# A depth-first forward pass in a fixed order on every engine, for a four-layer training step on one core

## The chip, the cores and the metric

One core of a Trainium2 chip runs the whole program, as one launch. The metric is the device time of that launch in microseconds (us). The core has a matrix engine (TensorE, here PE, with a separate row PEld for its weight loads), VectorE (DVE), ScalarE (ACT), GpSimd (POOL), and queues that issue DMAs; the one of SyncE (SP) issues nearly all of them here, ACT's a few.

## The reference

The input is one sequence of 2048 tokens with 512 features in bf16. Four layers follow one another: A, B, A, B, and both A layers share their weights, as do both B layers. The program returns the output and the gradients of the input and of the five weight matrices.

```
def _A_ref(x, wqkv, wo):
    H = 32; Dh = D // H
    qkv = (x @ wqkv).reshape(B, S, 3, H, Dh).transpose(2, 0, 3, 1, 4)
    q, k, v = qkv[0], qkv[1], qkv[2]
    phi = lambda t: jnp.where(t > 0, t + 1, jnp.exp(t)) + 1e-6
    pq, pk = phi(q), phi(k)
    kv = jnp.einsum("bhsd,bhse->bhde", pk, v)
    z = jnp.einsum("bhsd->bhd", pk)
    num = jnp.einsum("bhqd,bhde->bhqe", pq, kv)
    den = jnp.einsum("bhqd,bhd->bhq", pq, z)[..., None] + 1e-6
    return (num / den).transpose(0, 2, 1, 3).reshape(B, S, D) @ wo

def _B_ref(x, w_gate, w_up, w_down):
    g = jnp.einsum("bsd,df->bsf", x, w_gate)
    u = jnp.einsum("bsd,df->bsf", x, w_up)
    return jnp.einsum("bsf,fd->bsd", _sigmoid(g) * u, w_down)

x = x + _A_ref(_layernorm(x), A_wqkv, A_wo)
x = x + _B_ref(_layernorm(x), B_w_gate, B_w_up, B_w_down)
x = x + _A_ref(_layernorm(x), A_wqkv, A_wo)
x = x + _B_ref(_layernorm(x), B_w_gate, B_w_up, B_w_down)
```

F, the inner width of B, is 1376: ten chunks of 128 and one of 96. In A, kv and z are sums over all tokens, so no output of A can be made before every token's k and v are there.

## The kernel before

The tokens are 16 tiles of 128, or 4 blocks of 512. The residual stream stays in SBUF in f32 (one tile x per 128 tokens), and what the backward pass needs is stored to DRAM (sv_...). Layers 0 to 3 run one after the other.

The forward pass of an A layer (a_fwd) has three stages. First, for each tile: the layer norm (statistics on DVE, the reciprocal root in two small POOL operations, L291 and L292, the scaling on ACT, L295), four PE transposes into hT (L303), twelve wide matmuls for q, k and v (L402), two Exp on ACT, the min and max steps of phi on DVE, the copy of v on ACT, four more transposes of pq into pqT_all with an ACT copy, and stores of pq, pk and v by blocks. Second, once all tiles are through, z (L432) and kv (L438) are summed on PE in a stretch of their own. Third, for each tile: num and den (L455, L458), the division on DVE (L464), four transposes (L303) with an ACT copy to oT (L312), the product with wo (L476), a copy from PSUM on ACT (L479) and the residual add on POOL (L480).

The forward pass of a B layer (b_fwd) goes block by block: for each chunk of F four matmuls for g and four for u (L553, L556), two Sigmoid on ACT (L558, L560; the second is of -g), a product on DVE (L561) and one on POOL (L562). The product with w_down (L533) and the residual add on DVE (L535) of the block before are woven in at four chunks, together with the layer norms of the next block. sg, qg and hh are stored for each block.

The weights are loaded on SP at the start. After the forward pass their buffers are given back, and the backward pass loads transposed weights into that place with DMA transposes on SP (L201, L205, L206), then grad_out tiles. Its two kinds of phases are those that make gradients of activations (b_bwd_p1, a_bwd_p1) and those that make gradients of weights (b_bwd_p2, a_bwd_p2; L781, L811), the latter with transposed loads of p_set on SP (L757). In a_bwd_p1, BatchLoader (L631) loads two tiles of o and of pq at a time, two buffers each; pq is used by a DVE step (L932) and by PE (L921).

The order in which each engine works is chosen by the planner of the language at build time: it takes instructions by priority, in the order of the code, with a cost model, and may pull later ones forward. Within an engine's queue the result is fixed, and an instruction that waits holds all behind it.

Of the kernel before, what the change touches and what calls it, by code (L numbers as in the profile page):

```python
# [17 lines left out]
D = 512  # L18
# [32 lines left out]
def kernel(  # L51
# [43 lines left out]
    def load_stream(io, src2d, b):  # L95
        stg_t = io.tile([P, NB, D], BF16, name="io_in")
        if b == 0:
            nc.sync.dma_start(out=stg_t[:, 0, :], in_=src2d[0:P, :])
            nc.sync.dma_start(out=stg_t[:, 1:NB, :],
                              in_=src2d[P:NB * P, :].rearrange("(n p) d -> p n d", p=P))  # L100
        else:
            nc.sync.dma_start(out=stg_t[:], in_=dram_batch(src2d, b))
        for j in range(NB):
            st = b * NB + j
            if j % 2 == 0:
                nc.vector.tensor_copy(k.xs[st][:], stg_t[:, j, :])
            else:
                nc.scalar.copy(k.xs[st][:], stg_t[:, j, :])
        return stg_t
    k.load_stream = load_stream  # L110

    def store_stream(io, dst2d, b):
        stg_t = io.tile([P, NB, D], BF16, name="io_out")
        for j in range(NB):
            st = b * NB + j
            nc.gpsimd.tensor_scalar(stg_t[:, j, :], k.xs[st][:], 1.0, 0.0, ALU.mult, ALU.add)
        nc.sync.dma_start(out=dram_batch(dst2d, b), in_=stg_t[:])
    k.store_stream = store_stream


    k.sv = {}
    for l in range(4):
        d = {}
        d["h"] = dram.tile([S, D], BF16, name=f"sv_h{l}")
        d["gbf"] = dram.tile([S, D], BF16, name=f"sv_gbf{l}")
        if l % 2 == 0:
            for nm in ("pq", "pk", "v", "o"):
                d[nm] = dram.tile([S, D], BF16, name=f"sv_{nm}{l}")
            d["dqkv"] = dram.tile([S, 3 * D], BF16, name=f"sv_dqkv{l}")
        else:  # L130
            for nm in ("sg", "qg", "hh", "du", "dg"):
                d[nm] = dram.tile([F, S], BF16, name=f"sv_{nm}{l}")
        k.sv[l] = d
# [15 lines left out]
    with tc.tile_pool(name="wfwd", bufs=1) as wfwd:  # L149
        k.wqkv = wfwd.tile([P, NDC, 3 * D], BF16, name="wqkv")  # L150
        with tc.tile_pool(name="io0", bufs=2) as io:
            load_stream(io, x_in, 0)
            nc.sync.dma_start(out=k.wqkv[:], in_=A_wqkv.rearrange("(c p) j -> p c j", p=P))
            for b in range(1, NST // NB):
                load_stream(io, x_in, b)
        k.wo = wfwd.tile([P, NDC, D], BF16, name="wo")
        nc.sync.dma_start(out=k.wo[:], in_=A_wo.rearrange("(c p) j -> p c j", p=P))
        k.wg = wfwd.tile([P, NDC, F], BF16, name="wg")
        nc.sync.dma_start(out=k.wg[:], in_=B_w_gate.rearrange("(c p) j -> p c j", p=P))
        k.wu = wfwd.tile([P, NDC, F], BF16, name="wu")  # L160
        nc.sync.dma_start(out=k.wu[:], in_=B_w_up.rearrange("(c p) j -> p c j", p=P))
        k.wd = wfwd.tile([P, NFC, D], BF16, name="wd")
        nc.sync.dma_start(out=k.wd[:, 0:NFC - 1, :],
                          in_=B_w_down[0:(NFC - 1) * P, :].rearrange("(c p) j -> p c j", p=P))
        nc.sync.dma_start(out=k.wd[0:FLAST, NFC - 1, :], in_=B_w_down[(NFC - 1) * P:F, :])

        with ExitStack() as lctx:
            k.lnres = dict(
                stg=lctx.enter_context(tc.tile_pool(name="ln_stg", bufs=2)),
# [888 lines left out]
```

## Time and profile before

| What | us |
|---|---|
| median of 3 runs | 1398.83 (1398.69 to 1399.06) |
| the profiled execution, its time | 1398.62 |
| the profiled execution, its span | 1396.9 |
| PE busy in the span | 1234.9 (88%) |
| DVE, ACT, POOL busy | 666.1, 497.4, 250.2 |
| first matmul of layer 0 | 21.4 |
| first g matmul of layer 1 | 124.8 |
| first qkv matmul of layer 2 | 251.1 |
| first g matmul of layer 3 | 347.6 |
| last matmul of the forward pass ends | 465.8 |
| first PE work of the backward pass | 493.3 |

The span is the time from the first to the last instruction in the profile; the launch adds about 1.7 us to it. PE is busy for most of the span, but its busy time includes the tail of each pipelined matmul, so the text prices matmuls by the distance between the starts of two that follow one another. A line such as "PE tp L303 <- DVE ostage L464: 6.9, 9, 1.5" says that PE, before the instructions of line 303 that write tp, sat idle for 6.9 us in total in 9 places, the longest 1.5, until a DVE instruction of line 464 had written ostage. In the tables by stretch, the busy times of PE, PEld, DVE, ACT and POOL, each with its count of instructions, are followed by the granted clock of PE (1.00 is full), the busy share of the DMA engines and their GB/s.

### The profile page before, as it was taken

The page shows a single profiled execution, that of the slowest core. Times are in us where ns is not written, and L with a number is a line of the kernel's source. Part 1 is how long each engine was busy: PE and PEld are TensorE (multiplying, and loading weights), DVE is VectorE, ACT ScalarE, POOL GpSimd, SP SyncE. Part 2 cuts the span into 40 slices and gives each one's busy share as a digit, 9 for nine tenths or more (in the row PEclk, how much of TensorE's full clock was granted, in tenths as well). Part 3 has the DMA queues.
Part 4 walks back from the last instruction along what each step waited for, and adds up shares of the span by engine and source line. Part 5 has one row for each costly group of instructions (what it writes and reads, how often), then busy time and mean ns, then how long its engine had stood idle before and what let it go on. Part 6 is the DMA issues. An engine that isn't in the chain of part 4 may idle for free. (4 is left out here: it accounts for less than half of the span.)

```text
span 1396.9 us, 22644 instructions
## 1 busy us (share of the span) xinstructions
PE 1234.9 (88%) x8960; PEld 750.9 (54%) x8960; DVE 666.1 (48%) x1435; ACT 497.4 (36%) x871; POOL 250.2 (18%) x405
## 2 busy tenths in 40 slices
PE   3978999997999389998989889999989999749888
PEld 1454444454444156555745567655567665427657
DVE  6665565667443167666746200567513857301111
ACT  4846554656644122113457211111113457200000
POOL 4027555007644000011000100110101001000000
PEclk9989999999999789999999999999999999979999
DMA  8421355432444999969674897998687874799845
GB/s 279 166 75 62 122 167 192 164 114 91 152 137 137 261 288 304 243 162 254 162 203 137 179 222 160 291 269 229 165 255 226 219 195 164 195 242 214 177 118 157
DMA packets 469323, 263.70 MB, mean 189 GB/s; under 512 B 197728, under 2 KB 463584, under 8 KB 469216
## 3 DMA queue, kind: packets, MB, share of 16 engines
q1 hardware_dynamic: 446752, 247.57, 65.5%
q10 hardware_dynamic: 22464, 14.68, 3.8%
q8 instruction: 70, 1.15, 0.3%
q14 instruction: 37, 0.30, 0.1%
HBM read 98.37 MB, written 117.51 MB: 155 GB/s over the span
## 5 line engine op out<-in xcount | busy, mean ns | idle before, releaser
L781 PE MATMUL p_ps<-p_set,p_a 128*128 128x256 bf16 (+1 forms) x1920 | 210.8, 268 | 34.5 <-DMA p_set<-sv_dg 24.5
L781 PEld LDWEIGHTS <-p_a 128*128 128x128 bf16 x1920 | 173.8, 99 | 64.1 <-DMA p_set<-sv_dg 26.3
L580 ACT ACTIVATE t_sb<-dh_ps,rstd_all 128x512 f32<-128x512 f32 x64 | 44.0, 687 | 202.2 <-issue 114.7
L562 POOL TENSOR_TENSOR qg_t<-hh_t,oms 128x512 bf16<-128x512 bf16 (+1 forms) x88 | 101.1, 1152 | 80.1 <-DVE hh_t L561 74.0
L702 DVE TENSOR_TENSOR du_t<-dhh_ps,sg_ld 128x512 bf16<-128x512 f32 x96 | 61.2, 637 | 109.3 <-PE dhh_ps L700 109.3
L402 PE MATMUL mm_ps<-wqkv,hT 128*128 128x512 bf16 x384 | 94.8, 387 | 1.7 <-DVE x L535 1.7
L811 PE MATMUL p_ps<-p_a,p_set 128*128 128x512 bf16 (+1 forms) x352 | 84.8, 388 | 10.3 <-DMA p_set<-sv_hh 10.3
L561 DVE TENSOR_TENSOR hh_t<-u_ps,sg_t 128x512 bf16<-128x512 f32 (+1 forms) x88 | 60.4, 688 | 69.7 <-PE u_ps L556 50.0
L700 PE MATMUL dhh_ps<-gT,wdT 128*128 128x256 bf16 (+1 forms) x704 | 86.9, 276 | 7.5 <-DVE dg_t L704 6.2
L556 PE MATMUL u_ps<-hT,wu 128*128 128x512 bf16 (+1 forms) x352 | 90.3, 379 | 1.8 <-DVE hh_t L561 1.8
L553 PE MATMUL g_ps<-hT,wg 128*128 128x512 bf16 (+1 forms) x352 | 90.3, 379 | 1.6 <-DVE kvbdT L494 1.6
L582 DVE SCALAR_TENSOR_TENSOR junk<-t_sb,h_ld 128x512 bf16<-128x512 f32 x64 | 44.3, 692 | 96.2 <-ACT t_sb L580 96.2
L584 POOL TENSOR_SCALAR ab<-c 128x2 f32<-128x2 f32 x64 | 12.2, 191 | 418.4 <-DVE junk L582 418.4
L670 PE MATMUL dh_ps<-wuT,du_t 128*128 128x512 bf16 (+1 forms) x352 | 85.3, 383 | 0.3 <-DVE du_t L702 0.3
L670 PE MATMUL dh_ps<-wgT,dg_t 128*128 128x512 bf16 (+1 forms) x352 | 82.1, 380 | 0.0
L533 PE MATMUL y_ps<-wd,hh_t 128*128 128x512 bf16 (+1 forms) x352 | 81.6, 379 | 0.0
L700 PEld LDWEIGHTS <-wdT 128*128 128x128 bf16 (+1 forms) x704 | 68.3, 101 | 23.3 <-DVE dg_t L704 12.7
L610 POOL TENSOR_SCALAR gstage<-x 128x512 bf16<-128x512 f32 x48 | 32.0, 686 | 234.5 <-PE gT_ps L303 129.3
L786 DVE TENSOR_TENSOR dw_stg<-p_ps,dw_stg 128x512 bf16<-128x512 f32 (+1 forms) x36 | 23.5, 654 | 105.3 <-PE p_ps L781 99.9
L558 ACT ACTIVATE sg_t<-g_ps 128x512 bf16<-128x512 f32 (+1 forms) x88 | 52.3, 594 | 55.0 <-PE g_ps L553 54.9
L986 PE MATMUL dh_ps<-wqkvT,dkvT 128*128 128x512 bf16 x256 | 65.6, 380 | 0.0
L480 POOL TENSOR_TENSOR x<-y_sb,x 128x512 f32<-128x512 f32 x32 | 40.2, 1265 | 134.7 <-ACT y_sb L479 134.6
(158 smaller groups left out, 2041.8 us busy)
## 6 DMA issues: line engine op xcount, KB each, us to landing
sv_sg<-sg_t SPq DMA_DIRECT2D x8, 1280.0 KB, 5.7
sv_qg<-qg_t SPq DMA_DIRECT2D x8, 1280.0 KB, 7.8
sv_hh<-hh_t SPq DMA_DIRECT2D x8, 1280.0 KB, 9.2
sg_ld<-sv_sg SPq DMA_DIRECT2D x16, 640.0 KB, 5.5
qg_ld<-sv_qg SPq DMA_DIRECT2D x16, 640.0 KB, 6.3
sv_du<-du_t SPq DMA_DIRECT2D x16, 640.0 KB, 4.1
sv_dg<-dg_t SPq DMA_DIRECT2D x16, 640.0 KB, 5.6
sv_h<-hstage SPq DMA_DIRECT2D x16, 512.0 KB, 4.3
```

Of the source, the lines that this page charges most:

```text
L402: nc.tensor.matmul(ps[:], lhsT=hT[:, kc, :], rhs=k.wqkv[:, kc, n * D:(n + 1) * D], start=(kc == 0), stop=(kc == NDC - 1))
L533: nc.tensor.matmul(y_ps[:], lhsT=T["hh"][0:r, fc, j * P:(j + 1) * P], rhs=k.wd[0:r, fc, :], start=(fc == 0), stop=(fc == NFC - 1))
L553: nc.tensor.matmul(g_ps[0:r, :], lhsT=k.wg[:, kc, fs], rhs=hT[:, kc, :], start=(kc == 0), stop=(kc == NDC - 1))
L556: nc.tensor.matmul(u_ps[0:r, :], lhsT=k.wu[:, kc, fs], rhs=hT[:, kc, :], start=(kc == 0), stop=(kc == NDC - 1))
L561: nc.vector.tensor_tensor(T["hh"][0:r, fc, :], u_ps[0:r, :], T["sg"][0:r, fc, :], ALU.mult)
L562: nc.gpsimd.tensor_tensor(T["qg"][0:r, fc, :], T["hh"][0:r, fc, :], oms[0:r, :], ALU.mult)
L670: nc.tensor.matmul(dh_ps[:], lhsT=T[nm][0:r, fc, j * P:(j + 1) * P], rhs=wT[0:r, fc, :], start=(i == 0), stop=(i == n_mm - 1))
L700: nc.tensor.matmul(dhh_ps[0:r, i, :], lhsT=k.wdT[:, jc, fc * P:fc * P + r], rhs=gT[:, jc, :], start=(jc == 0), stop=(jc == NDC - 1))
L702: nc.vector.tensor_tensor(T["du"][0:r, fp:fp + n, :], dhh_ps[0:r, 0:n, :], sg[0:r, fp:fp + n, :], ALU.mult)
L781: nc.tensor.matmul(psv[:, icl, :], lhsT=lhs_all[:, st, ic * P:(ic + 1) * P], rhs=set_t[:, st, 0:W], start=(st == 0), stop=(st == NST - 1))
L811: nc.tensor.matmul(ps[0:r, :], lhsT=st_t[:, st, j * P:j * P + r], rhs=g_all[:, st, :], start=(st == 0), stop=(st == NST - 1))
L986: nc.tensor.matmul(dh_ps[:], lhsT=lhsT, rhs=k.wqkvT[:, n * NDC + c, :], start=(i == 0), stop=(i == 3 * NDC - 1))
```

## The change

The forward pass is a new class, Forward. Its instructions are issued within a manual schedule: every engine runs them in the order in which the code makes them, with no planner. The backward pass is planned as before.

- Head: the x tiles are loaded into a staging buffer; the layer norm reads that buffer, and POOL makes the f32 copy. The thirds of wqkv for k and v are loaded by ACT's queue, the one for q by SP. A loop staggers the tiles: in step i the statistics of tile i, the scaling of tile i-1, the transposes of tile i-2, the k and v matmuls of tile i-3 and the kv sums of tile i-4.
- kv and z are summed in two PSUM banks that stay open, tile by tile (acc_tile), while k and v are made. For layer 2 this goes on between the blocks of layer 1 (k_block, v_acc).
- q is made by blocks with the weights as the stationary operand, so that it comes out as pqT, 128 features by 512 tokens; it is neither transposed on PE nor kept for the whole sequence. It is stored as pqT.
- phi takes its min step on POOL in place of DVE, 512 columns at a time.
- Depth first: block sb of layer B follows as soon as block sb of layer A is out; o_block of the next block, the kv sums and the last steps of kv are woven between its matmuls. drive() picks, at build time, the stream that is least far along among those whose modelled latency is over, with 217 ns for a wide matmul and 57 for a square one; the second number of each yield is the latency in ns that it assumes.
- The attention's residual add reads PSUM directly on DVE; the ACT copy y_sb and the POOL add are gone.
- All small PSUM tiles share six buffers in turn. sg and qg are stored for every two chunks from a ring of three buffers, hh for each block.
- In a_bwd_p1, pq is loaded from sv_pqT by DMA transposes (TransLoader), two tiles at a time.

gu_block, not shown, has the matmuls, Sigmoids and products of b_fwd; k_tile and v_tile have the k and v matmuls; kv_finish masks the sums into rhsN and kv_extra makes the forms that the backward pass needs.

```diff
-            for nm in ("pq", "pk", "v", "o"):
+            for nm in ("pk", "v", "o"):
                 d[nm] = dram.tile([S, D], BF16, name=f"sv_{nm}{l}")
+            d["pqT"] = dram.tile([D, S], BF16, name=f"sv_pqT{l}")
...
-            lns = [FwdLN(k, l) for l in range(4)]
-            a_fwd(k, 0, lns[0], nxt=lns[1])
-            b_fwd(k, 1, lns[1], nxt=lns[2])
-            a_fwd(k, 2, lns[2], nxt=lns[3])
...
-            b_fwd(k, 3, lns[3], out_cb=out_cb)
+    with ExitStack() as fctx:
+        Forward(k, fctx, x_in, A_wqkv, A_wo, B_w_gate, B_w_up, B_w_down, out0).run()
...
+def drive(streams, t=0.0):
+    live = [dict(g=g, tot=tot, done=0.0, ready=t) for g, tot in streams]
+    while live:
+        ok = [s for s in live if s["ready"] <= t]
+        s = min(ok, key=lambda s: s["done"] / s["tot"]) if ok else min(live, key=lambda s: s["ready"])
+        t = max(t, s["ready"])
+        try:
+            cost, lat = next(s["g"])
+        except StopIteration:
+            live.remove(s)
+            continue
+        t += cost
+        s["done"] += cost
+        s["ready"] = t + lat
...
+        self.p_hh = pool("f_hh", 2)
+        self.p_ring = pool("f_ring", 3)
+        self.ps = pool("f_ps", 6, space=PSUM)
...
+    def phi(self, dst, ps):
+        nc = self.nc
+        e_t = self.p_ea.tile([P, D], BF16, name="e_t")
+        nc.scalar.activation(e_t[:], ps, ACT.Exp)
+        a_t = self.p_e2.tile([P, D], BF16, name="a_t")
+        nc.gpsimd.tensor_scalar(a_t[:], e_t[:], 1.0, EPS, ALU.min, ALU.add)
+        return lambda: nc.vector.scalar_tensor_tensor(dst, ps, 1.0 + EPS, a_t[:], ALU.add, ALU.max)
+    def q_block(self, l, sb):
+        nc = self.nc
+        hT = self.hA.pop((l, sb))
+        t = self.p_pq.tile([P, NDC, SB], BF16, name="pqT")
+        self.pq[l, sb] = t
+        late = None
+        for c in range(NDC):
+            ps = self.ps_tile("q_ps")
+            for kc in range(NDC):
+                nc.tensor.matmul(ps[:], lhsT=self.wqkv[:, kc, c * P:(c + 1) * P], rhs=hT[:, kc, :],
+                                 start=(kc == 0), stop=(kc == NDC - 1))
+            nxt = self.phi(t[:, c, :], ps[:])
+            if late is not None:
+                late()
+            late = nxt
+            yield NDC * MM, 0
+        late()
+        yield 0, 3000
+        nc.sync.dma_start(out=self.k.sv[l]["pqT"][:, sb * SB:(sb + 1) * SB].rearrange("(c p) s -> p c s", p=P),
+                          in_=t[:])
...
+    def acc_tile(self, l, st):
+        k, nc = self.k, self.nc
+        sb, j = divmod(st, NB)
+        pk, v = self.kvt[l, sb]
+        last = st == NST - 1
+        for c in range(NDC):
+            cs = slice(c * P, (c + 1) * P)
+            nc.tensor.matmul(self.kv_ps[:, c, :], lhsT=pk[:, j, cs], rhs=v[:, j, cs], start=False, stop=last,
+                             skip_group_check=True)
+            nc.tensor.matmul(self.z_ps[:, c:c + 1], lhsT=pk[:, j, cs], rhs=k.ones_col[:], start=False, stop=last,
+                             skip_group_check=True)
...
+    def o_tile(self, l, st):
+        k, nc = self.k, self.nc
+        sb, j = divmod(st, NB)
+        kv = k.kv[l]
+        pq = self.pq[l, sb][:, :, j * P:(j + 1) * P]
+        if j == 0:
+            self.ost = self.p_o.tile([P, NB, D], BF16, name="ostage")
+        ost = self.ost
+        num = self.ps_tile("num_ps")
+        den = self.ps_tile("den_ps", (P, H))
+        for c in range(NDC):
+            nc.tensor.matmul(den[:, c * 8:(c + 1) * 8], lhsT=pq[:, c, :], rhs=kv["rhsN"][:, c, P:P + 8],
+                             start=True, stop=True)
+            nc.tensor.matmul(num[:, c * P:(c + 1) * P], lhsT=pq[:, c, :], rhs=kv["rhsN"][:, c, 0:P],
+                             start=True, stop=True)
+        rden = kv["rden_all"][:, st, :]
+        dtmp = self.small.tile([P, H], F32, name="dtmp")
+        nc.vector.tensor_scalar(dtmp[:], den[:], EPS, None, ALU.add)
+        nc.vector.reciprocal(rden, dtmp[:])
+        o_t = ost[:, j, :]
+        nc.vector.tensor_tensor(o_t.rearrange("p (h e) -> p h e", h=H), num[:].rearrange("p (h e) -> p h e", h=H),
+                                rden.unsqueeze(2).to_broadcast([P, H, DH]), ALU.mult)
+        yield NDC * 84, 1800
+        tp = self.ps_tile("o_tp", (P, NDC, P), BF16)
+        for c in range(NDC):
+            nc.tensor.transpose(tp[:, c, :], o_t[:, c * P:(c + 1) * P], k.ident[:])
+        oT = self.p_oT.tile([P, NDC, P], BF16, name="oT")
+        nc.scalar.copy(oT[:], tp[:])
+        if j == NB - 1:
+            nc.sync.dma_start(out=dram_batch(k.sv[l]["o"], sb), in_=ost[:])
+        yield NDC * TR, 1000
+        y = self.ps_tile("y_ps")
+        for c in range(NDC):
+            nc.tensor.matmul(y[:], lhsT=oT[:, c, :], rhs=self.wo[:, c, :], start=(c == 0), stop=(c == NDC - 1))
+        nc.vector.tensor_tensor(k.xs[st][:], y[:], k.xs[st][:], ALU.add)
+        yield NDC * MM, 1000
+        yield from self.ln(l + 1, st, k.xs[st][:])
+        yield from self.hT(l + 1, st)
+        if j == NB - 1:
+            self.store_h(l + 1, sb)
...
+    def o_block(self, l, sb):
+        gens = [self.o_tile(l, sb * NB + j) for j in range(NB)]
+        live = []
+        ready = {}
+        t = 0.0
+        while gens or live:
+            if gens and len(live) < 3:
+                g = gens.pop(0)
+                live.append(g)
+                ready[id(g)] = t
+            g = min(live, key=lambda g: (ready[id(g)]))
+            wait = max(0.0, ready[id(g)] - t)
+            if wait > 0:
+                yield 0, wait
+            t += wait
+            try:
+                c, lat = next(g)
+            except StopIteration:
+                live.remove(g)
+                continue
+            t += c
+            ready[id(g)] = t + lat
+            yield c, 0
...
+    def y_block(self, l, sb, last=False):
+        k, nc = self.k, self.nc
+        pend = []
+        if last:
+            ot = self.p_o.tile([P, NB, D], BF16, name="out0_t", tag="ostage")
+        for j in range(NB):
+            st = sb * NB + j
+            self.y_tile(l, st)
+            yield NFC * MM, 0
+            if last:
+                nc.scalar.copy(ot[:, j, :], k.xs[st][:])
+                continue
+            pend.append(self.ln(l + 1, st, k.xs[st][:]))
+            for g in list(pend):
+                try:
+                    next(g)
+                except StopIteration:
+                    pend.remove(g)
+        self.hh.pop((l, sb))
+        if last:
+            yield 0, 2000
+            nc.sync.dma_start(out=dram_batch(self.out0, sb), in_=ot[:])
+            return
+        while pend:
+            yield 0, 2000
+            for g in list(pend):
+                try:
+                    next(g)
+                except StopIteration:
+                    pend.remove(g)
+        yield 0, 1000
+        for j in range(NB):
+            yield from self.hT(l + 1, sb * NB + j)
+        self.store_h(l + 1, sb)
...
+        load_x(0)
+        for n in (1, 2):
+            nc.scalar.dma_start(out=self.wqkv[:, :, n * D:(n + 1) * D], in_=self.w_in["wqkv"][:, :, n * D:(n + 1) * D])
+        load_x(1)
+        nc.sync.dma_start(out=self.wqkv[:, :, 0:D], in_=self.w_in["wqkv"][:, :, 0:D])
...
+        for i in range(n + 4):
+            if i < n:
+                sb, j = divmod(i, NB)
+                x_ap = xt[sb][:, j, :]
+                lns[i] = self.ln(0, i, x_ap)
+                next(lns[i])
+            if 1 <= i <= n:
+                next(lns[i - 1])
+                sb, j = divmod(i - 1, NB)
+                nc.gpsimd.tensor_copy(k.xs[i - 1][:], xt[sb][:, j, :])
+            if 2 <= i <= n + 1:
+                for _ in self.hT(0, i - 2):
+                    pass
+                if (i - 2) % NB == NB - 1:
+                    self.store_h(0, (i - 2) // NB)
+            if 3 <= i <= n + 2:
+                late[i - 3] = self.k_tile(0, i - 3)
+                self.v_tile(0, i - 3)
+            if 4 <= i:
+                late.pop(i - 4)()
+                if i < n + 3:
+                    self.acc_tile(0, i - 4)
+                    if (i - 4) % NB == NB - 1:
+                        self.store_kv(0, (i - 4) // NB)
+                if (i - 4) % NB == 0:
+                    late_loads((i - 4) // NB)
+        for _ in self.q_block(0, 0):
+            pass
+        self.acc_tile(0, n - 1)
+        self.store_kv(0, NSB - 1)
+    def run(self):
+        k, tc = self.k, self.k.tc
+        with tc.manual_schedule():
+            self.head()
+            for l in (0, 2):
+                self.kv_finish(l)
+                if l == 0:
+                    drive([(self.q_block(0, 1), self.Q_COST), (self.o_block(0, 0), self.O_COST)])
+                    self.kv_start(2)
+                else:
+                    drive([(self.o_block(2, 0), self.O_COST), (self.q_block(2, 1), self.Q_COST)])
+                for sb in range(NSB):
+                    early = []
+                    if l == 0 and sb >= 1:
+                        early.append((self.k_block(2, sb - 1), self.K_COST))
+                    if sb + 2 < NSB:
+                        early.append((self.q_block(l, sb + 2), self.Q_COST))
+                    main = [(self.b_block(l + 1, sb, last=(l == 2)), self.B_COST)]
                     if sb + 1 < NSB:
+                        main.append((self.o_block(l, sb + 1), self.O_COST))
+                    if l == 0 and sb >= 1:
+                        main.append((self.v_acc(2, sb - 1), self.V_COST))
+                    if sb == 0:
+                        main.append((self.kv_extra(l), 2 * NDC * TR))
+                    drive(early)
+                    drive(main)
+                if l == 0:
+                    drive([(chain(self.k_block(2, NSB - 1), self.v_acc(2, NSB - 1)), self.K_COST + self.V_COST),
+                           (self.q_block(2, 0), self.Q_COST)])
...
+class TransLoader:
+    def __init__(self, k, pool, srcT, name, nb):
+        self.k, self.pool, self.srcT, self.name, self.nb = k, pool, srcT, name, nb
+        self.cur = None
+    def get(self, st):
+        nb = self.nb
+        if st % nb == 0:
+            self.cur = self.pool.tile([P, nb, D], BF16, name=self.name)
+            self.k.nc.sync.dma_start_transpose(out=self.cur[:], in_=self.srcT[:, st * P:(st + nb) * P])
+        return self.cur[:, st % nb, :]
...
-            pqld = BatchLoader(k, stg, sv["pq"], "pq_ld", nb=NB2)
+            pqld = TransLoader(k, stg, sv["pqT"], "pq_ld", nb=NB2)
```

## The prediction

> **What bounds the kernel now.** I read the busy digits in 40 slices first, then the busy time by stage, then what TensorE (PE) waited for, then the timeline at both ends of the forward pass, and single rows for prices.
>
> ```profile
> PE   3978999997999389998989889999989999749888
> PEclk9989999999999789999999999999999999979999
> 20.00:77.00 57.00, 53.56 (x320) 25.63 (x320) 38.65 (x90) 45.89 (x80) 7.17 (x18) 1.00 0.53 182
> 77.00:84.00 7.00, 6.71 (x128) 6.68 (x127) 2.42 (x13) 0.58 (x1) 0.00 (x0) 0.76 0.66 227
> 84.00:124.00 40.00, 30.34 (x286) 18.52 (x284) 24.86 (x78) 23.00 (x39) 23.80 (x31) 0.91 0.21 71
> 124.00:244.00 120.00, 114.25 (x572) 53.44 (x571) 64.60 (x136) 63.89 (x110) 68.17 (x87) 1.00 0.43 142
> 244.00:302.00 58.00, 54.94 (x341) 26.44 (x339) 36.44 (x73) 39.09 (x69) 2.97 (x8) 1.00 0.43 145
> 309.00:345.00 36.00, 27.75 (x255) 16.54 (x256) 26.10 (x83) 22.87 (x40) 24.40 (x34) 0.95 0.21 73
> 345.00:466.00 121.00, 117.78 (x579) 55.24 (x577) 49.17 (x89) 62.73 (x113) 58.06 (x59) 1.00 0.48 157
> ```
>
> After the stretch and its length come the busy times of PE, weight loads, DVE, ACT and POOL. ACT reaches 81% in the first stretch and no other engine as much anywhere, so PE sets the pace. It loses little in the qkv and gated stages, and a quarter of the time in the two stretches that make the attention output (84 to 124, 309 to 345). Slice 14 is a hole: the hand-over to the backward pass.
>
> ```profile
> 21.36 0.60 PE L303 MATMUL ln_tp<-ident,hstage 128*128 128x128 bf16 x4 [21.36 <-ACT hstage L295]
> PE ln_tp L303 <- ACT hstage L295: 22.5, 3, 21.4
> PE tp L303 <- DVE ostage L464: 6.9, 9, 1.5
> 456.14 9.68 PE L533 MATMUL y_ps<-wd,hh_t 128*128 128x512 bf16 x44
> 467.69 8.33 SPq L201 DMA_TRANSPOSE wdT<-in_B_w_down_dram  x1
> 493.29 0.58 PE L303 MATMUL gT_ps<-ident,gstage 128*128 128x128 bf16 x4 [27.48 <-DMA gstage<-in_grad_out_dram]
> ```
>
> PE starts at 21.4, though x first landed by 6.2 (the first DVE cast): ACT casts later tiles first. The forward pass ends on PE at 465.8; 27.5 us follow while the transposed backward weights are issued on SP.
>
> **What PE must do.** Four wide matmuls start 0.86 us apart (435.19 to 436.05), eleven take 2.38: 0.216 us each. Before there are 704 for g and u, 352 for the gated output, 384 for qkv and 128 for wo: 1568 x 0.216 = 338.7. Square ones (four transposes, then the next start 0.23 later) cost 0.057: 784 x 0.057 = 44.7. The narrow den and z ones take 0.026 (64 in 1.60): 256 x 0.026 = 6.7. Sum 390; PE took 444.4 (21.4 to 465.8), so 54 are lost, and 21.4 passed before it.
>
> **The change, part by part.**
>
> *q transposed.* q comes out as pqT, with as many wide matmuls; 128 transposes go: -7.3, so 382.8 remain. Their 32 ACT copies (0.58 each) go too.
>
> *Head.* x is normalised straight from the staging tile, in tile order. From 6.2: statistics 0.69 + 0.18, POOL 0.50 + 0.57, nmr 0.20, hstage 0.81, transposes 0.40, copy 0.41 = 3.8, hand-overs 0.3, other tiles' DVE steps ahead in the queue 1.2: first k matmul at 11.5. The k and v thirds of wqkv go out on ACT's DMA queue ahead of its first activation; the whole took 7.7 us to land, so they are there. Per tile then: PE 8 x 0.216 + 8 x 0.057 + 4 x 0.026 = 2.29; DVE 0.68 + 0.17 + 0.21 + 0.41 + 0.69 = 2.16; ACT 0.81 + 0.60 + 0.59 = 2.0; POOL 0.23 + 0.57 plus two ops of a form not in the trace (x cast bf16 to f32, a_t). The nearest rows for these are the POOL cast L610 (0.62) and the two-input ops (1.15 and 1.27): POOL 2.04 to 3.22. I take 0.62, one input each, and a pace of 2.5: 40 us. With q_block(0,0), 16 x 0.216 = 3.5, the head ends at 55. At 3.22 it ends 11.5 later.
>
> *The rest of the work* is 382.8 - 16 x 2.29 - 3.5 = 342.7.
>
> *Waits that the fixed order adds.* (1) In layer 0 each of four blocks ends with the layer norm of its last gated tile, and PE stands at its transposes with the next block's k_block and q_block queued behind. The chain by rows: add 0.69, statistics 0.65 + 0.17, POOL 0.30 + 0.56, nmr 0.20, hstage 0.82, hops 0.3: 3.7, less the three earlier tiles' transposes (0.7): 3 each, 12; between 6 (other streams' leftovers fill it) and 24 (DVE late with the interleaved tile). (2) o_block(l,0) has only q_block(l,1) beside it, and three tiles live: the fourth starts when the first is done. A tile's chain is 0.45 + 1.2 + 0.4 + 0.6 + 0.9 + 3.7 + hops 0.4 = 7.7, two rounds 15.4, for 16 x 0.216 + 4 x 1.66 = 10.1 of PE: 5.3 twice, and 1.5 for kv_finish in layer 2: 12; between 8 and 20. (3) Small waits elsewhere: 345 to 466 holds 535 wide and 40 square matmuls, 117.9 priced (2.6% lost), 124 to 244 510 and 58, 113.5 (5.7%). I take 4% of 342.7: 14; between 9 and 20. (4) The clock: 80 to 82 ran at 0.50, 100 to 106 at 0.5 after some 3 us of near idleness. One or two such spells: 3; between 0 and 6. Sum 41, between 23 and 70.
>
> The Trainium skill ("TensorE: Matmul & The Clock Gate", Part 1) has the clock fall to half after an idle window of about 3.4 us, and recover after as long a busy one; if each of the six waits did that at 1.7 us lost, the sum would rise by some 7 us above the 3 taken here.
>
> *Forward pass:* 55 + 342.7 + 41 = 439 on PE, against 465.8: -27.
>
> *Taken at nothing.* The attention residual moves from ACT and POOL (0.59 + 1.27) to DVE (0.69 from PSUM): 32 x 0.69 = 22 more on DVE, which has 246 busy of 446 now; a_t leaves it (-13.6). POOL gains 64 x 0.62. The kv sums leave their own stretches (7 us each, already priced). PE covers all this; a full block of layer 0 has 196 x 0.216 + 80 x 0.057 + 32 x 0.026 = 47.7 of PE; DVE has 39 steps of about 0.69, eight copies of 0.41 and some 5 us of small ones, 35. Without that cover DVE would bind there. SP gets 14 store issues a block in place of 6, 64 more at 0.4 to 1.2; it only holds up later stores there. The two weight reloads in slice 14 stay behind the last out store, so the 27.5 stay. Exp and Sigmoid now alternate by block: I count 11 table loads after the first, against 3, so 8 x 1.283 = 10 us of ACT, which with its 258 now less the two kinds of copies (38) is busy for 230 of 439. PE runs on for some five us in six PSUM buffers meanwhile; if not, 10 us.
>
> The skill's "ScalarE: Activation LUTs" (Table sets: the hidden batching unit) says to do all of one set before the next, which speaks against this change, and puts a switch at about 2.7 us with its drain. By the page ACT gets 22 us, by the row 10; the row stands, and either hides behind PE.
>
> *Backward pass.* pq_ld becomes a DMA transpose, 16 loads of 512x256. Issue on SP: 0.42 now; transposes of 512x128 take 1.25, of 512x512 2.79, so between: 1.8. That is 1.4 x 8 per layer on SP, ahead of o_ld, gbf stores and the p_set transposes that PE waits for.
>
> ```profile
> L757 SPq DMA_TRANSPOSE p_set<-sv_du x12: 1285/4307/9212, 641.6 to 1318.0; - x12
> L206 SPq DMA_TRANSPOSE wuT<-wtail_wu x2: 1247/1250/1253, 481.8 to 789.6; - x2
> L631 SPq DMA_DIRECT2D pq_ld<-sv_pq x16: 359/419/522, 633.6 to 1109.0; - x16
>   DVE dphq L932: 4.3, 4
> ```
>
> Two buffers and 6 us between loads hide most of it. Lower end 0, upper end all of one layer's, 11; SP has gaps from 660 on, so +3.
>
> **Sum.** The profiled execution took 1398.62 (span 1396.9; median of the runs 1398.83, no difference that matters). 1398.7 - 27 + 3 = 1375. All terms at their good ends (pace 2.29, waits 23, backward 0) give 1350; all at their bad ends, 1423.
>
> **Rivals.**
>
> *PE nearly full.* If real latencies are shorter than the order assumes, waits shrink to 15 and the pace to 2.29: 51.6 + 342.7 + 15 = 409, -57: 1342. For it: PE loses 2.6% in the last stretch. Against: the layer-norm chain at block ends is real work on four engines.
>
> *In-order stalls at every tile, slower.* PE now stands at each tile's transposes until DVE and ACT deliver, with everything behind it held. 84 to 124 has 24.1 us of priced work: 15.9 lost over 16 tiles, 1.0 a tile, half clock included. If the 32 attention tiles and the 16 layer norms after the gated layer lose as much, 48 replaces 14: +34, 1409. It decides from 0.8 us a tile, where the gain of 24 is gone. For it: that stretch has just these chains. Against: there nothing else was at hand for PE, and now gated matmuls stand between.
>
> *The lost time only moves.* The earlier start (10) and the transposes (7) come back as block-end waits at their upper end (+12) and a POOL-bound head (+11.5): 1375 + 23.5, about 1399.
>
> **How the numbers follow.** Forecast 0.60 (its own range 1350 to 1396), PE nearly full 0.12, stalls 0.20, moved 0.08. The time is the forecast's, 1375; 1346 to 1409 takes in most of the first three. A measurement here can't tell less than 0.2% (2.8 us) from no change. Faster: 0.60 + 0.12 + 0.02 of the moved case = 0.74. Within: 0.05 of the moved case + 0.01 of the stalls = 0.06. Slower: 0.20.
>
> **What would show it.** First k matmul near 11.5 and head end near 55; last gated matmul near 439, then the same 27 us hole; PE waits of about 3 us on hstage at four block ends of layer 0 and some 5 us around the first o_block of each layer; no clock digit below 9 between; twelve table loads in all; pq_ld issues of 1.8 us and no new PE wait around 640. POOL above 2.5 us a tile in the head, tile waits above 0.8 us, or PE waiting for pq_ld would make the prediction wrong.

## The result, and the profile after

The changed kernel takes **1486.94 us** (median of 4 runs, 1480.27 to 1492.26) against 1398.94 for the kernel before on the same chip: the ratio is 1.0625, 95% interval 1.0572 to 1.0677. It is slower by 88 us, and above the predicted range. The profiled execution took 1480.27 us, the least of the four; its span is 1478.5, 81.6 more than before.

The busy digits of the page, first for the kernel after:

```profile
PE   5658688886779883999898989999999999959988
PEclk9969898898789997999999999999999999979999
```

Each digit is 37 us now. In the first sixteen PE is mostly below 9, and the clock is below 9 in eight of them. Before, the clock was below 9 in four slices of all forty, and PE mostly at 9 or 8. The busy times by stage for the kernel after (length, then PE, weight loads, DVE, ACT and POOL, granted clock, DMA share, GB/s): the head; the first o_block; layers 0 and 1; the first o_block of layer 2; the rest.

```profile
20.00:70.00 50.00, 36.33 (x291) 18.51 (x292) 24.19 (x59) 27.03 (x42) 45.58 (x51) 1.00 0.63 210
70.00:109.00 39.00, 19.99 (x109) 9.79 (x108) 18.91 (x45) 8.86 (x15) 17.64 (x16) 0.65 0.24 81
109.00:352.00 243.00, 202.77 (x1131) 99.51 (x1130) 119.48 (x254) 111.24 (x178) 124.63 (x128) 0.89 0.33 109
352.00:385.00 33.00, 18.99 (x113) 9.33 (x113) 16.27 (x38) 9.24 (x15) 13.68 (x14) 0.69 0.38 128
385.00:561.00 176.00, 149.07 (x793) 71.14 (x791) 84.41 (x167) 80.86 (x137) 72.44 (x75) 0.91 0.39 130
```

In the head POOL is busy for 45.58 of 50 us and PE for 36. After that no engine is full: something is being waited for. What PE waited for in the forward pass of the kernel after:

```profile
PE h_tp L375 <- ACT hstage L363: 53.2, 14, 10.8
PE o_tp L543 <- DVE ostage L538: 18.0, 8, 3.0
PE kv_ps L465 <- DVE pk_t L389: 13.6, 13, 1.1
PE den_ps L529 <- DVE rhsN L491: 7.4, 2, 6.5
PE v_ps L435 <- DVE pk_t L389: 6.9, 4, 3.0
```

Of the 53.2 only 10.8 is the start. Two kinds of waits stand out: on the layer norm and the division of attention tiles (hstage, ostage), and on phi (pk_t). The timeline of PE at the two ends of the hand-over, after:

```profile
551.53 9.68 PE L640 MATMUL y_ps<-wd,hh_t 128*128 128x512 bf16 x44
562.08 0.38 PE L228 MATMUL gT_ps<-ident,gstage 128*128 128x128 bf16 x4 [0.87 <-DVE x L642]
575.98 2.99 PE L928 MATMUL dhh_ps<-gT,wdT 128*128 128x256 bf16 x16 [0.67 <-ACT gT L237]
```

The forward pass ends on PE at 561.2 (551.53 + 9.68), 95.4 later than before. From there to the first dhh it is 14.8, where it was 30.1 (465.8 to 495.9): 15.3 back. From the first dhh to the end of the span it is 902.5, where it was 901.0. 95.4 - 15.3 + 1.5 = 81.6: in this execution the loss is all in the forward pass.

### The profile page after: what moved, and what is told of

It reads as the page before. It is cut to its first block, busy times and chain, and to the rows that moved or that the text cites. A ratio compares the mean times of both kernels' runs of the same rounds, so it can differ in the third digit from the quotient of the medians.

```text
span 1478.5 us, 22487 instructions
## 1 busy us (share of the span) xinstructions
PE 1261.0 (85%) x8832; PEld 754.9 (51%) x8832; DVE 680.3 (46%) x1413; ACT 477.9 (32%) x807; POOL 343.8 (23%) x453
## 5 line engine op out<-in xcount | busy, mean ns | idle before, releaser
L388 POOL TENSOR_SCALAR a_t<-e_t 128x512 bf16<-128x512 bf16 x64 | 123.5, 1930 | 43.9 <-ACT e_t L386 38.2
L604 PE MATMUL g_ps<-hT,wg 128*128 128x512 bf16 (+1 forms) x352 | 96.0, 398 | 2.0 <-DVE hT L376 1.0
L607 PE MATMUL u_ps<-hT,wu 128*128 128x512 bf16 (+1 forms) x352 | 93.7, 390 | 1.8 <-DVE pk_t L389 1.0
L640 PE MATMUL y_ps<-wd,hh_t 128*128 128x512 bf16 (+1 forms) x352 | 77.4, 379 | 0.0
L375 PE MATMUL h_tp<-ident,hstage 128*128 128x128 bf16 x256 | 27.3, 259 | 53.6 <-ACT hstage L363 53.2
L363 ACT ACTIVATE hstage<-x,ln_nmr,rstd_all 128x512 bf16<-128x512 f32 x48 | 37.9, 810 | 107.0 <-DVE ln_nmr L359 107.0
```

The lines of the kernel that those rows point to most:

```text
L388: nc.gpsimd.tensor_scalar(a_t[:], e_t[:], 1.0, EPS, ALU.min, ALU.add)
L604: nc.tensor.matmul(g_ps[0:r, :], lhsT=self.wg[:, kc, fs], rhs=hT[:, kc, :], start=(kc == 0), stop=(kc == NDC - 1))
L607: nc.tensor.matmul(u_ps[0:r, :], lhsT=self.wu[:, kc, fs], rhs=hT[:, kc, :], start=(kc == 0), stop=(kc == NDC - 1))
L640: nc.tensor.matmul(y[:], lhsT=hh[0:r, fc, j * P:(j + 1) * P], rhs=self.wd[0:r, fc, :], start=(fc == 0), stop=(fc == NFC - 1))
```

## The experiments

Two theories. **P**: the min step of phi, moved to POOL, costs much more than taken, and sets the pace wherever k or q is made. **O**: the fixed order itself makes PE stand, at the ends of its chains, and the clock falls there. The first edits are each made to the changed kernel, and one to the kernel before; from the kernel with both steps on DVE late on, edits are added to one another, and each section names the kernel that it starts from. Runs that are not in the table are given in their sections. Where the forward pass ends on PE is read from the last y_ps row, the head's end from the first q_ps row; the clock is the mean from 20 us to that end (21 for the kernel before).

| Run | us | ratio to before (95%) | first q_ps | forward ends | clock |
|---|---|---|---|---|---|
| before | 1398.94 | | | 465.8 | 0.98 |
| after | 1486.94 | 1.0625 (1.0572 to 1.0677) | 65.6 | 561.2 | 0.88 |
| min step on DVE, at once | 1438.48 | 1.0302 (1.0283 to 1.0321) | 63.6 | 512.8 | 0.91 |
| mult for min on POOL | 1421.85, one run | | 48.9 | 495.7 | 0.92 |
| both steps on DVE, late | 1428.54 | 1.0221 (1.0191 to 1.0251) | 49.4 | 499.5 | 0.90 |
| the same, with idle matmuls | 1404.11, one run | | | 484.3 | 0.98 |
| fillers | 1415.45 | 1.0115 (1.0080 to 1.0150) | | 489.8 | 0.92 |
| better order | 1369.60 | 0.9770 (0.9742 to 0.9797) | 49.1 | 446.1 | 0.97 |
| better order, min on POOL | 1438.78 | 1.0275 (1.0243 to 1.0307) | 65.6 | 513.0 | 0.93 |

**The min step on DVE.**

```diff
-        a_t = self.p_e2.tile([P, D], BF16, name="a_t")
-        nc.gpsimd.tensor_scalar(a_t[:], e_t[:], 1.0, EPS, ALU.min, ALU.add)
-        return lambda: nc.vector.scalar_tensor_tensor(dst, ps, 1.0 + EPS, a_t[:], ALU.add, ALU.max)
+        nc.vector.tensor_scalar(e_t[:], e_t[:], 1.0, EPS, ALU.min, ALU.add)
+        return lambda: nc.vector.scalar_tensor_tensor(dst, ps, 1.0 + EPS, e_t[:], ALU.add, ALU.max)
```

> The changed kernel with the min step of phi (a_t) back on DVE, in place in the tile e_t, which gets a fourth buffer. Theory P (POOL: a_t at 1.93 us sets the pace of the head, of the q and k blocks and of the start of the attention output, and the waits it makes let the clock fall): the head's pace falls from 3.56 to about 2.5 us a tile (-17), the start of the attention output from some 38 to 17 us in each A layer (-40), the q and k blocks between lose their waits (-25): about 1400, and below it if the clock stays up. Theory O (order: the fixed order's own waits at the ends of tile chains, with the half clock that follows them, cost most): only the waits that the profile books to a_t and what hangs on it go, some 45 us in all, and the clock stays near 0.87 between 100 and 500: 1440 or more.

It took 1438.48, 48 less. The groups of the min step, in the kernel after (POOL) and in this run (DVE), with count, busy time, mean ns and the idle time before them:

```profile
L388 POOL TENSOR_SCALAR a_t<-e_t 128x512 bf16<-128x512 bf16 x64 | 123.5, 1930 | 43.9 <-ACT e_t L386 38.2 <-DVE pk_t L389 1.8
```

```profile
L387 DVE TENSOR_SCALAR e_t<-e_t 128x512 bf16<-128x512 bf16 x64 | 19.2, 300 | 42.4 <-ACT e_t L386 42.4
```

The same step takes 1.93 us on POOL and 0.30 on DVE. But DVE now stands for 42.4 us until ACT's Exp is done, with all its other work held behind, so the head is hardly shorter (q at 63.6). The run shows less than the whole price; by its number it stands with theory O (1440 or more), not with P (about 1400).

**Another operation on POOL in its place.**

```diff
-        nc.gpsimd.tensor_scalar(a_t[:], e_t[:], 1.0, EPS, ALU.min, ALU.add)
+        nc.gpsimd.tensor_scalar(a_t[:], e_t[:], 1.0, EPS, ALU.mult, ALU.add)
```

> The changed kernel with a_t on POOL as mult and add in place of min and add; this leaves the min out, so phi is another function. If the operation min is what makes a_t slow, its mean falls from 1.93 to near 0.62 us, the mean of the cast on POOL, and the kernel falls to the time of the run with a_t on DVE (about 1400 by P). If bf16 in and out with two operations is what costs, a_t stays near 1.9 and the time at 1480 to 1490.

It took 1421.85, 65 less than the median after, with all else the same, instruction by instruction. The group in this run:

```profile
L388 POOL TENSOR_SCALAR a_t<-e_t 128x512 bf16<-128x512 bf16 x64 | 39.5, 618 | 62.8 <-ACT e_t L386 56.5 <-DVE pqT L389 2.5 <-DVE pk_t L389 1.9
```

0.618 in place of 1.930, with the same shape, type, count and neighbours: on POOL it is the min that costs. The head is 16.7 shorter, the whole forward pass 65.5. It still ends 30 us later than before (495.7 against 465.8), and the time is not P's 1400: theory P is not all.

**The planner in place of the fixed order.**

```diff
-        with tc.manual_schedule():
+        if True:
```

> The changed kernel with its forward pass ordered by the planner in place of the fixed order; a_t stays on POOL. Theory O: the planner fills the waits, the time falls well below 1487, to 1400 to 1420. Theory P: POOL still needs 3.4 us a tile in the head and 1.93 for each q and k chunk, so the time stays above 1450 whatever the order.

It took 1501.6 (one run), above P's 1450, where O had 1400 to 1420. PE waited 57.6 for hstage and 22.6 for ostage, more than in the fixed order (53.2 and 18.0). With the min step on POOL, the planner makes no better order out of this code than the one written out; the later edits try other sequences.

**The kernel before, with the min step on POOL.**

```diff
-                nc.vector.tensor_scalar(a_t[:], e_t[:], 1.0, EPS, ALU.min, ALU.add)
+                for hf in range(2):
+                    nc.gpsimd.tensor_scalar(a_t[:, hf * D:(hf + 1) * D], e_t[:, hf * D:(hf + 1) * D], 1.0, EPS, ALU.min, ALU.add)
```

> The kernel before with a_t alone moved to POOL, as two instructions of 512 columns. Theory P: 64 instructions of 1.93 us make each qkv stage POOL-bound, 16 x (2 x 1.93 + 0.80) = 75 us against 58 now: +34, about 1433. If a planned order hides a slow POOL (Theory O): within 10 us of before.

It took 1452.1 (one run) against 1397.03, 55 more, and more than P's 34, so the price is there without any other part of the change. The wait in this run:

```profile
PE tp L303 <- DVE pqstage L412: 47.7, 32, 2.5
```

Each of the 32 tiles holds PE at the transposes of pq for 1.5 us.

**Both steps of phi on DVE, issued late.** DVE no longer stands at Exp, and POOL has neither step.

```diff
+        def late():
+            nc.vector.tensor_scalar(e_t[:], e_t[:], 1.0, EPS, ALU.min, ALU.add)
+            nc.vector.scalar_tensor_tensor(dst, ps, 1.0 + EPS, e_t[:], ALU.add, ALU.max)
+        return late
```

> As the changed kernel, but both steps of phi on DVE, and the first of them issued only when the second is, a half later, so that DVE does not stand at Exp. Theory P (the price of the min step on POOL, and the waits that it makes, cost most): POOL is out of the chain and DVE has about as much slack as POOL had with the cheap operation: 1415 to 1425, the head ends by 53. Theory O (the order's own waits at the ends of chains and the half clock after them cost most): little of the remaining loss moves against the 1438 with the min step on DVE in place: 1430 to 1440.

1428.54, between the two theories' numbers (P to 1425, O from 1430) and nearer to O's. The edit also gives e_t a fourth buffer, as the run with the min step on DVE had. The forward pass ends 61.7 earlier than after. The remaining PE waits are those of theory O, and they have not moved:

```profile
PE h_tp L375 <- ACT hstage L363: 50.2, 14, 10.7
PE o_tp L545 <- DVE ostage L540: 18.0, 8, 3.0
```

The next edits start from this kernel. **The clock of the latencies.** o_block reckons when a tile is ready on a clock that counts only its own steps; here it uses that of drive.

```diff
+CLK = [0.0]
...
+        CLK[0] = t
...
-            wait = max(0.0, ready[id(g)] - t)
+            wait = max(0.0, ready[id(g)] - CLK[0])
...
-            ready[id(g)] = t + lat
+            ready[id(g)] = CLK[0] + c + lat
```

> As the run before it, but o_block reckons its tiles' latencies on the clock of drive in place of its own, which leaves out the time given to the other streams. Theory O: the fourth tile of each block then starts as soon as a place is free and no longer trails alone; PE's waits for hstage and ostage at the ends of the 8 o_blocks lose 1 to 2 us each and the clock recovers with them: 10 to 25 us less than the run before. Theory P: the placing is no cause, within 5 us of it.

1434.89 (ratio 1.0264, 1.0235 to 1.0292): no gain, some 6 us more. Theory O's expectation fails, and the waits of this run show where:

```profile
PE h_tp L379 <- ACT hstage L367: 76.6, 20, 10.8
PE o_tp L549 <- DVE ostage L544: 2.9, 3, 1.3
```

The fourth tile's division is now covered (18.0 to 2.9), but PE waits 26 us more at the transposes of the layer norm (50.2 to 76.6). The reading, which this run alone does not show, is that the order trusts latencies that are too short, and an earlier tile only meets them earlier. One such place (103 to 115) fits it: DVE's step after the reciprocal root (ln_nmr) starts 5.6 us after the statistics of that tile, where the order assumed 2.6.

**Idle matmuls where PE waits** (from the kernel at 1428.54).

```diff
+    def dummy(self, n):
+        for _ in range(n):
+            self.nc.tensor.matmul(self.z_ps[:, 16:512], lhsT=self.wo[:, 0, 0:P], rhs=self.wo[:, 1, 16:512],
+                                  start=False, stop=False, skip_group_check=True)
...
+        if j == NB - 1:
+            self.dummy(8)
...
+        if j == NB - 1 or (sb == 0 and j == 0):
+            self.dummy(12)
```

> As the first run of this job, with matmuls that compute nothing used (496 columns each, into spare columns of a bank): 8 before the transposes of each block's fourth attention tile, 12 before the layer-norm transposes of each fourth tile and of the very first. They take about 0.21 us each, some 20 us in all, mostly where PE waits. If the half clock after the waits is a cost of its own, the clock stays up and the time falls by 10 to 20 us; if only the waits cost, it is the same or up to 15 us longer.

The edit adds 184 matmuls (9016 for 8832), 38 us at an estimated 0.209 each (0.216 x 496/512), more than the expectation's text reckons. The time fell all the same by 24, to 1404.11: the forward pass ends 15.2 earlier, and some 6 of the rest lie in the backward pass, which the edit doesn't touch. The forward pass as one window, without and with them:

```profile
20.00:499.00 479.00, 407.77 (x2424) 204.04 (x2422) 277.49 (x621) 236.51 (x386) 153.07 (x215) 0.90 0.42 140
```

```profile
20.00:485.00 465.00, 429.46 (x2604) 215.47 (x2602) 277.41 (x620) 236.18 (x385) 152.91 (x215) 0.98 0.43 144
```

The clock is 0.98 in place of 0.90, as in the kernel before. 0.10 x 479 = 48 us of clock were not granted without them, 9 with them. Not all of the 48 is lost, as PE was partly idle then: summed over windows of 1 us, 27 us of it, and 10 with them, fell while PE was busy. PE's busy time agrees: 429.5 less the 38 of the idle matmuls is some 391, against 407.8 for the same work. So the half clock after the waits is a cost of its own.

**Fillers** (from the kernel with drive's clock). k_block, v_acc and q_block of later blocks, and kv_extra, run only where the streams on the path are not ready.

```diff
-        s = min(ok, key=lambda s: s["done"] / s["tot"]) if ok else min(live, key=lambda s: s["ready"])
+        s = min(ok, key=lambda s: (s["f"], s["done"] / s["tot"])) if ok else min(live, key=lambda s: s["ready"])
...
-                    drive(early)
-                    drive(main)
+                    drive(main, fill=fill)
```

> As the second run of this job, with k_block, v_acc and q_block of later blocks used only where the streams that the path waits for are not ready, in place of running in step with them, and what is left of them at the end. Theory O: the waits at block ends are covered by that work and another 10 to 25 us go, to 1375 to 1400. Theory P: no gain beyond 5 us. A third way: the fillers are used up before the block's end, where the waits are, and nothing is gained.

1415.45: 19 less than the run it starts from. That is the drop that theory O had (10 to 25), but not its 1375 to 1400, since the run before had brought no gain. PE still waits 63.6 for hstage, so the fillers can't be the whole cure.

**A better order** (from the fillers): longer latencies, four live attention tiles, o_block earlier. Not shown are 1.5 us for 1.0 in y_block and a fourth buffer of oT.

```diff
-        yield 0, 2600
+        yield 0, 3300
...
-        yield 0, 1400
+        yield 0, 1800
...
-            yield 0, 2000
+            yield 0, 2800
...
-            if gens and len(live) < 3:
+            if gens and len(live) < 4:
...
-                        main.append((self.o_block(l, sb + 1), self.O_COST))
+                        main.append((self.o_block(l, sb + 1), 1.6 * self.O_COST))
```

> As the run with fillers, with latencies nearer to the rows given to the order (3.3 and 1.8 us for the two halves of a layer norm in place of 2.6 and 1.4; 2.8 us a step at the end of the gated block in place of 2.0), four attention tiles live in place of three, and o_block put earlier beside the gated block (its share counted 1.6 times as large), so that its last tile has gated matmuls beside it. Theory O (the order's own waits): PE's waits for hstage fall from 52.8 us past the first to 25 or less, and the time to 1375 to 1400. If the fillers are used up early, the waits move to the block ends and the time is within 10 us of 1415.

**1369.60, below the kernel before** (ratio 0.9770, 0.9742 to 0.9797), and 59 below the kernel with phi on DVE late. Waits and clock of the forward pass in this run:

```profile
PE h_tp L379 <- ACT hstage L367: 32.6, 22, 10.9
...
PE o_tp L549 <- DVE ostage L544: 1.7, 4, 0.5
```

```profile
20.00:446.00 426.00, 389.86 (x2379) 197.50 (x2420) 275.55 (x621) 235.13 (x388) 152.85 (x215) 0.97 0.47 157
```

Past the start 22 us are left for hstage, 13 of them at the two first o_blocks. The clock has come back with no idle matmul.

**Idle matmuls in the better order**, wherever the order expects a wait.

```diff
+        if pad is not None and s["ready"] > t:
+            pad(int((s["ready"] - t) / MM))
```

> As the run before it, with matmuls that compute nothing used (0.21 us each, 202 of them) wherever the order expects PE to wait. If the half clock after waits still costs, 5 to 20 us less than that run; if the waits are too few or too short to bring the clock down, the same or up to 15 us more. Below 1397 it beats the kernel before.

1394.31, 25 more, where 15 was expected at most; the forward pass ends 24 later. 202 of them cost some 42 us, and with a clock of 0.97 there is little to win back. Here they do not pay.

**The min step back on POOL, in the better order.**

> As the run with the better order at 1369.6, with the min step of phi on POOL again as in the changed kernel, at 1.93 us a time (and 7 buffers in place of 8 for the small statistics). The head alone, at POOL's pace, ends some 16 us later. Theory O (the order's own waits were the larger part): only that and little more comes back, 1383 to 1395, still below the kernel before. Theory P (the price of the min step cost most, in every block): 1420 to 1440, as the 58 between the changed kernel and the one with both steps on DVE late.

1438.78, 69 more: what theory P said. (e_t has three buffers again and the small statistics seven; neither was tried alone.) DVE's waits in this run:

```profile
DVE pk_t L394 <- POOL a_t L393: 60.1, 29, 4.8
DVE pqT L394 <- POOL a_t L393: 38.4, 22, 3.1
```

Of the 69 the forward pass has 66.9, the head alone 16.4. The rest is paid block by block; that it comes from what DVE holds back while it stands at a_t is read from these waits.

**o_block at its own share again.**

> As the run with the better order at 1369.6, but o_block's share beside the gated block counted at its own size again, so that both end together. If the place of o_block made the gain from 1415, the time is 1395 to 1415; if the longer latencies and the fourth live tile made it, within 10 us of 1370.

1387.72 (1378.28 to 1390.28; ratio 0.9891, 0.9841 to 0.9942), between the two expectations. From the fillers' 1415 to here, 28, is the longer latencies and the fourth tile together, with its buffer; from here to 1369.6, 18, the place of o_block.

## Why the prediction was wrong

Forward was to end at 439 on PE and ended at 561.2, 122 later. The kernel with phi on DVE late ends at 499.5, which splits this into 61.7 for POOL's min step and 60.5 for waits and clock.

**Head: the price of a_t is the step that failed first.** The sum took 0.62 from the cast row and set the upper bound at 1.27, the dearest two-input row. It takes 1.93, above the bound. POOL in the head of the kernel after, by its timeline:

```profile
28.31 0.61 POOL L736 CAST x<-x_in 128x512 f32<-128x512 bf16 x1
29.00 1.95 POOL L388 TENSOR_SCALAR a_t<-e_t 128x512 bf16<-128x512 bf16 x1
31.03 0.23 POOL L355 TENSOR_SCALAR rstd_all<-ln_mv 128x1 f32<-128x1 f32 x1
31.34 0.57 POOL L356 TENSOR_TENSOR rstd_all<-rstd_all,neghalf 128x1 f32<-128x1 f32 x1
31.87 0.61 POOL L736 CAST x<-x_in 128x512 f32<-128x512 bf16 x1
```

One tile is 3.56 us (28.31 to 31.87) and POOL is busy for 3.4 of it. The cast's 0.61 was right. With the cheap operation the head is as predicted: q_ps at 48.9 and 3.5 for it gives 52.4, against 55. The first k matmul came at 12.1, against 11.5.

**"Taken at nothing": POOL's 64 steps.** The text priced a pace set by POOL for the head alone, and took PE to cover POOL's steps in the blocks. POOL's load over the forward pass (274 of 541 us) does not show the cost. A step of 1.9 us in a chain of PE, ACT, POOL and DVE holds DVE in order, and through it PE. DVE's waits for it, after:

```profile
DVE pk_t L389 <- POOL a_t L388: 59.1, 32, 3.9
DVE pqT L389 <- POOL a_t L388: 44.5, 28, 3.9
```

Its price is 61.7 of the forward pass in all, some 16 of it in the head.

**Waits, terms (1) to (3): the place and the size were off.** Term (1) put 3 us at the ends of the four gated blocks of layer 0. Most of the waits stand at the end of each o_block instead, in both A layers, where the fourth attention tile trails alone. PE's timeline there, after:

```profile
153.38 0.40 PE L543 MATMUL o_tp<-ident,ostage 128*128 128x128 bf16 x4 [2.98 <-DVE ostage L538]
154.82 1.77 PE L551 MATMUL y_ps<-wo,oT 128*128 128x512 bf16 x4 [1.04 <-ACT oT L545]
...
160.56 0.40 PE L375 MATMUL h_tp<-ident,hstage 128*128 128x128 bf16 x4 [2.27 <-ACT hstage L363]
```

Each link waits for the one before it: 2.98 + 1.04 + 2.27 = 6.3, and 6.1 to 6.7 at the five other block ends, some 38 where 12 were taken. In the kernel with phi on DVE late the waits at the first o_blocks are 13.2 and 12.0, 25 in all (term (2): 12, at most 20), and what is left of its 70 us of waits, 7, is below term (3)'s 14. In all, 70 stand against 38.

**Term (4), the clock: 3 us taken, 6 at most.** In windows of 4 us after the stretch just shown:

```profile
158.00:162.00 4.00, 1.73 (x13) 0.82 (x12) 2.04 (x7) 2.23 (x3) 0.77 (x2) 0.93 0.14 47
162.00:166.00 4.00, 4.00 (x13) 1.48 (x12) 0.69 (x1) 1.65 (x3) 3.38 (x2) 0.60 0.24 84
```

PE is busy for all of the last window and gets 0.60. By windows of 1 us the clock is 0.50 from 155 to 158 and from 162 to 165. In the forward pass 0.12 x 541 = 65 us were not granted in the kernel after, 48 with phi on DVE late; 43 and 27 of them while PE was busy, and only those can have cost time.

Of the 60.5 above, 32 are waits beyond the 38, and 2 were gained in the head (its end at 52.9, q_ps at 49.4 and 3.5). The other 31, and the 3 taken here, are time in which PE is busy beyond its price: from the head's end on it is busy for 375.3 where 342.7 was priced. At most 27 us of that busy time can be the clock; some 16 of it went when idle matmuls held the clock at 0.98 (15 off the forward pass, net of their own time). What the rest is stays open; the kernel before, with its clock at 0.98, was also busy for longer (411.6) than its priced 390.

The Trainium skill ("TensorE: Matmul & The Clock Gate", Part 1) was cited against the change for 7 us at six waits; it has the clock halve after an idle window of about 3.4 us. In these rows no wait is that long (2.98 at most), but in the 3.5 us before 155 PE was busy for only 0.6, and in the 3.7 before 162 for 1.4: waits with a few matmuls between them were enough. What was wrong was the count: the kernel with phi on DVE late has sixteen waits of 2 us or more past the start, and sixteen at the 1.7 us of that sentence are 27, an estimate that meets the 27 above.

**The hole.** "The 27.5 stay" failed, in the kernel's favour. From the last y_ps to the first dhh it is 14.8. In the kernel after the queue's timeline has:

```profile
559.82 4.18 SPq L985 DMA_TRANSPOSE p_set<-sv_hh  x1
564.09 5.34 SPq L139 DMA_TRANSPOSE wdT<-in_B_w_down_dram  x1
569.52 0.53 SPq L666 DMA_DIRECT2D out_dram<-out_t  x1
```

wdT goes out ahead of the last out store, not behind it, and the first grad_out tiles were fetched long before (from 357 on). What is left of the hole is the reverse wait: ACT's first copy of gT stands until that out store has landed.

```profile
574.09 0.58 ACT L237 COPY gT<-gT_ps 128x512 bf16<-128x512 bf16 x1 [11.50 <-DMA out_dram<-out_t]
```

The planner of the backward pass may place such loads earlier now that the forward pass is in another schedule; the prediction took the old places for granted. Why they moved was not tried.

**Backward pass: right in the profiled execution.** +3 (0 to 11) was forecast, +1.5 came. In the other edited forms of the changed kernel, whose backward code is the same, this stretch took 902.4 to 916.0, so 1.5 lies within what varies. The issue of pq_ld takes 1.27, not 1.8, and DVE's waits rise by 1.2 (4.3 before):

```profile
L862 SPq DMA_TRANSPOSE pq_ld<-sv_pqT x16: 1229/1267/1914, 721.9 to 1196.1; - x16
  DMA pq_ld<-sv_pqT: 5.5, 4
```

**Table loads: right.** There are twelve (6 + 5 + 1, each 1.283), as counted, and no wait in PE's list names them. By ACT's timeline each of the eleven after the first stands right before an Exp or a Sigmoid, and none before a scaling to hstage or a copy to oT, so none lies inside PE's waits for those.

**The rivals.** "In-order stalls at every tile" had the right sign. Its mechanism, some 1 us at each of 48 attention and layer-norm tiles, is not what the rows show: their waits are few and long, at the ends of chains (waits of 1.1 us at each tile stand in the head, for pk_t behind POOL's step). "The lost time only moves" had the POOL-bound head, at 11.5, where some 16 came. A gain of the size that was forecast is there to be had, but by another kernel than the one predicted: with phi on DVE and the better order, the forward pass ends at 446.1 and the kernel takes 1369.6.

## What to carry to other kernels

Price a moved step by a row with the same operation on the same engine; another operation of the same form is no bound for it. In a chain over four engines such a step costs by its latency where something in order stands behind it (61.7 us here), and the engine's total load (274 of 541) does not show this. Before you trust an order written out by hand, look for the last unit of each group: give its steps latencies no shorter than the rows, start it early enough that other work is left beside it, and price the clock beside the waits: here 70 us of waits went with up to 27 of lost clock, an estimated 1.7 for each wait of 2 us or more.

## What was not expected of the hardware

- A tensor_scalar over 128x512 in bf16 on POOL takes 1.93 us with min and add (the kernel after) and 0.618 with mult and add; on DVE the one with min and add takes 0.300.
- Matmuls that compute nothing used can shorten a kernel: 184 of them (38 us) took 15 us off the forward pass by holding the clock at 0.98 in place of 0.90, and 202 of them added 24 where the clock was already at 0.97.
